# Attention plus gated MLP on one core: transposes of the next batch moved beside the output product, the MLP's first half left alone, all masks on VectorE, and a reordered start

## The chip, the cores and the metric

The kernel runs on one core of one Trainium2 chip. The metric is the device time of one execution in microseconds (us). The profile's span is 1.7 to 1.9 us shorter than the device time, because it leaves out launch and end; times inside an execution are counted from the start of that span.

A core has five engines with separate instruction queues. PE (TensorE) multiplies matrices and, against an identity matrix, transposes. DVE (VectorE) and ACT (ScalarE) do elementwise work. POOL (GpSimd) can do elementwise work too, and here it also issues nearly all loads. SP (SyncE) issues the stores. PE writes to PSUM, everything else lies in SBUF.

## The reference

Eight batches, each with eight heads of attention (576 positions, 64 numbers per head) and then one gated MLP block. Heads 0 to 3 look back over 32 positions; heads 4 to 7 over 128 positions, every fourth one.

```python
scores = q @ k.T / sqrt(64)          # masked: band of 32, or 32 steps of 4
attn   = softmax(scores) @ v         # [8, 8, 576, 64]
x      = heads side by side          # [8, 576, 512]
h      = gelu(x @ w_in)              # [8, 576, 1024]
u, v   = h[..., :512], h[..., 512:]
v_n    = layernorm(v) * g_ln
v_s    = w_sg @ v_n + b_sg           # mixes the 576 positions
out    = x + (u * v_s) @ w_out
```

## The kernel before

One batch is worked on per pass `p`, and the gate and the output product of batch `p-1` are woven in. The stages are written as strings that set the program order of every engine. `S:h` is scores, exp and mask of a head. `sgu` is the gate product, its scaled result `vs` and the product `gat`. `AV` is the weighted sum with its normalised result `onorm`. `X` transposes `onorm` into `xT`. `out` is the output product. `T:g` transposes q and k of two heads of the next batch into `qT` and `kT` (`kI` for the dilated heads). `zv` and `zu` are the two halves of `x @ w_in`. `vn` normalises. `W` transposes w_sg, in pass 0 only.

```python
        # a_S, the end of a head's scores
        nc.scalar.activation(PT[:, 0:S]..., pss[:, :, 0:HS], AF.Exp, scale=0.125)
        eng = nc.gpsimd if b and h % 4 == 3 else nc.vector      # masks of heads 3, 7 on POOL
        eng.tensor_tensor(PT[:, 0:S], PT[:, 0:S], masks[:, h // 4], AO.mult)
        ...
        # m_sgu, the end of a gate product
        nc.vector.scalar_tensor_tensor(vs..., pv[:, :, 0:HS], g_col[:, ph:ph + 1], b_bc..., AO.mult, AO.add)
        nc.vector.tensor_tensor(gat[:, ph, :], u[:, ph, :], vs, AO.mult)
        ...
        # m_zv, after gelu: statistics on DVE, then 1/sqrt(var) as rs on POOL
        nc.gpsimd.tensor_scalar_add(rs[:, 0:n], mv[:, 0:n, 1:2], 1e-6)
        nc.gpsimd.tensor_tensor(rs[:, 0:n], rs[:, 0:n], mhalf[:, 0:n], AO.pow)
        ...
    for p in range(B + 1):
        ...
        # io: loads, spread evenly between the steps of a string
        run("S:0 sgu:0 S:1 S:2 sgu:1 S:3 S:4 sgu:2 S:5 sgu:3 S:6 S:7 gelu", env, io)
        ...
        run("AV:0 vd AV:1 out:0 X:0 AV:2 X:1 out:1 AV:3 X:2 T:0 X:3 out:2", env, io)
        ...
        run("zv:0 T:1 zv:1 vn:0 W:0 T:2 zv:2 vn:1 W:1 zu:0 vn:2 T:3 zu:1 W:2 zu:2 W:3 zu:3 W:4", env, io)
```

All PSUM results share one pool of four slots, so a result that is copied out late also holds up a later product. The weight transposes, the first q and k, and all loads of pass 0 are written before or inside the same strings.

The softmax here doesn't subtract the row's maximum and nothing guards it: scores larger than these inputs give would overflow.

Of the kernel before, what the change touches and what calls it, by code (L numbers as in the profile page):

```python
# [11 lines left out]
FP16 = mybir.dt.float16  # L12
AF = mybir.ActivationFunctionType
AO = mybir.AluOpType

B, H, S, D = 8, 8, 576, 64
DM, DFF, DH = 512, 1024, 512
# [8 lines left out]
NB, QB, KB, HALO = 6, 96, 128, 32  # L26
# [27 lines left out]
def kernel(  # L54
# [12 lines left out]
    nc = tc.nc  # L67
# [6 lines left out]
    sb = ctx.enter_context(tc.tile_pool(name="sb", bufs=2))  # L74
# [7 lines left out]
    masks = const.tile([KB, 2, S], FP16)  # L82
# [7 lines left out]
    warm = const.tile([128, 1], FP32)  # L90


    NKT = 3
    kTs = [[const.tile([128, HALO + S], FP16, name=f"kT{i}_{hd}") for hd in range(2)]
           for i in range(NKT)]

# [3 lines left out]
    NV = 2  # L100
    vps = [const.tile([KB, 4, NB, 66], FP16, name=f"vp{i}") for i in range(NV)]
    vds = [const.tile([KB, 4, NB, 66], FP16, name=f"vd{i}") for i in range(NV)]
    NPT = 10
    PTb = [const.tile([KB, PTW], FP16, name=f"PT{i}") for i in range(NPT)]

    def setup_consts():
        nc.sync.dma_start(ident16, IDT.ap())
        nc.sync.dma_start(masks, MSK.ap())
        nc.vector.memset(mhalf, -0.5)
        for i in range(NKT):  # L110
            for hd in range(2):
                nc.vector.memset(kTs[i][hd], 0.0)
            nc.vector.memset(kIs[i], 0.0)
        for t in vps + vds:
            nc.vector.memset(t[0:HALO], 0.0)
            nc.vector.memset(t[:, :, :, 64:65], 1.0)
        for t in PTb:
            nc.vector.memset(t[:, S:PTW], 1.0)
        nc.vector.memset(wsgT16[0:64, 4, :], 0.0)


    def dma(dst, src):
        nc.gpsimd.dma_start(dst, src)  # L123

    loaded = {}

    def open_batch(b):
        qp = ld.tile([QB, NB, 4, D], FP16, tag="qp", name="qp")
        kp = ld.tile([QB, NB, 4, D], FP16, tag="kp", name="kp")
        qd = ld.tile([TB, 4, 2, 4, D], FP16, tag="qd", name="qd")  # L130
        kd = ld.tile([TB, 4, 2, 4, D], FP16, tag="kd", name="kd")
        loaded[b] = ((qp, kp), (qd, kd))

    def ld_plain(b, h0):
        if h0 == 0:
            open_batch(b)
        for t, src in zip(loaded[b][0], (q, k)):
            for h in range(h0, h0 + 2):
                dma(t[:, :, h, :], src[b][h].rearrange("(a p) d -> p a d", p=QB))

    def ld_dil(b):
        for t, src in zip(loaded[b][1], (q, k)):
            dma(t.rearrange("p h f r d -> p (h f) (r d)"),
                src[b][4:8].rearrange("h (f p r) d -> p (h f) (r d)", p=TB, r=4))
# [24 lines left out]
        nc.vector.tensor_copy(vd[:, :, 4:6, 0:D], vt[:, :, 0:3:2, :])  # L169

    def ld_win():
        dma(w_in16, moe_w_in.rearrange("(g p) f -> p g f", p=128))

    def ld_wsg():
        dma(wsg16, moe_w_sg.rearrange("(a p) s -> p a s", p=QB))
# [51 lines left out]
    def a_S(b, h):  # L227
        qT, kT = qkT[b, h // 2]
        pss = psum("pss")
        if h < 4:  # L230
            kx, qx = kT[h % 2], qT.rearrange("p j w -> p (j w)")
            for a in range(NB):
                nc.tensor.matmul(pss[:, a // 3, QB * (a % 3):QB * (a % 3) + QB],
                                 kx[:, QB * a:QB * a + KB], qx[:, QB * a:QB * a + QB],
                                 start=True, stop=True)
        else:
            for j in range(2):
                kx = kT[:, h % 2, NM * j:NM * j + NM, :]
                qx = qT[:, h % 2, NM * j:NM * j + NM]
                for r in range(2):  # L240
                    nc.tensor.matmul(pss[:, j, 128 * r:128 * r + 128],
                                     kx[:, 0:KB, r], qx[:, 0:128], start=True, stop=True)
                nc.tensor.matmul(pss[:, j, 256:HS], kx[:, NM - 64:NM, :],  # L243
                                 qx[:, 128:NM].unsqueeze(1).broadcast_to([128, 2, 16]),
                                 start=True, stop=True)
        PT = PTb[(8 * b + h) % NPT]
        nc.scalar.activation(PT[:, 0:S].rearrange("p (j w) -> p j w", j=2),  # L247
                             pss[:, :, 0:HS], AF.Exp, scale=0.125)
        eng = nc.gpsimd if b and h % 4 == 3 else nc.vector
        eng.tensor_tensor(PT[:, 0:S], PT[:, 0:S], masks[:, h // 4], AO.mult)  # L250
        PTs[b, h] = PT

    def a_AV(b, g):
# [23 lines left out]

    def a_X(b, g):
        onorm = onorms.pop((b, g))
        if g == 0:  # L280
            xTs[b] = sb.tile([128, 4, S], FP16, tag="xT", name="xT", bufs=4)
        xT = xTs[b]
        pxt = psum("pxt")
        if g < 2:
# [21 lines left out]
    def m_zv(b, i):  # L306
# [10 lines left out]
                                 start=(g4 == 0), stop=(g4 == 3))  # L317
        vv = sb.tile([128, 2, DH], FP32, tag="vv", name="vv", bufs=3)
        nc.scalar.activation(vv[:, 0:n], pz[:, 0:n], AF.Gelu_apprx_tanh)  # L319
        st = sb.tile([128, 2, 6], FP32, tag="st", name="st", bufs=3)  # L320
        mv = sb.tile([128, 2, 2], FP32, tag="mv", name="mv", bufs=3)
        rs = sb.tile([128, 2, 1], FP32, tag="rs", name="rs", bufs=3)
# [63 lines left out]
    def gelu_table():  # L386
        nc.scalar.activation(warm, mhalf[:, 0, :], AF.Gelu_apprx_tanh)

    LOADS = {"qk": lambda b: [(ld_plain, b, 0), (ld_plain, b, 2), (ld_dil, b)],
             "v": lambda b: [(ld_vp, b, 0, 4), (ld_vd, b)]}  # L390

    def run(text, env, io):

        steps = text.split()
        done = 0
        for i, step in enumerate(steps):
            while done < len(io) and done * len(steps) <= i * len(io):
                f, *a = io[done]
                f(*a)
                done += 1  # L400
            name, _, n = step.partition(":")
            if name in env:
                f, *a = env[name]
                f(*a, *([int(n)] if n else []))
        for f, *a in io[done:]:
            f(*a)

    setup_consts()
    for f, *a in LOADS["qk"](0) + LOADS["v"](0):
        f(*a)  # L410
    ld_win()
    for g in range(4):
        a_T(0, g)
    for p in range(B + 1):
        env = {"gelu": (gelu_table,)}
        if p < B:
            env |= {"S": (a_S, p), "AV": (a_AV, p), "X": (a_X, p), "vd": (cp_vd, p),
                    "zv": (m_zv, p), "vn": (m_vn, p), "zu": (m_zu, p)}
        if p + 1 < B:
            env["T"] = (a_T, p + 1)  # L420
        if p == 0:
            env["W"] = (prep_wsg,)
        if p >= 1:
            env |= {"sgu": (m_sgu, p - 1), "out": (m_out, p - 1)}
        if p == 0:
            io = LOADS["qk"](1) + [(ld_wsg,)]
        else:
            io = LOADS["v"](p + 1) if p + 1 < B else []
        run("S:0 sgu:0 S:1 S:2 sgu:1 S:3 S:4 sgu:2 S:5 sgu:3 S:6 S:7 gelu", env, io)
        io = LOADS["v"](1) + [(ld_wout,)] if p == 0 else []  # L430
        run("AV:0 vd AV:1 out:0 X:0 AV:2 X:1 out:1 AV:3 X:2 T:0 X:3 out:2", env, io)
        io = LOADS["qk"](p + 2) if p + 2 < B else []
        run("zv:0 T:1 zv:1 vn:0 W:0 T:2 zv:2 vn:1 W:1 zu:0 vn:2 T:3 zu:1 W:2 zu:2 W:3 zu:3 W:4",
            env, io)


# [28 lines left out]
```

## Time and profile before

| | before |
|---|---|
| device time, median (range) | 289.38 us (289.23 to 290.4) |
| span of the profile | 287.8 us |
| pass 0: start to the first scores of pass 1 | 52.89 us |
| a steady pass (first scores to next first scores) | 31.70 us |
| from the first scores of the last attention pass to the end | 45.64 us |

Two sections of the profile page of the kernel before follow: the span with each engine's busy time (its share, and after x its instructions), and the span cut into 40 slices of 7.2 us, in which a digit is the busy share in tenths and PEclk the granted TensorE clock in tenths.

```profile
span 287.8 us, 6135 instructions
PE 234.7 (82%) x2494; PEld 167.4 (58%) x2494; DVE 198.7 (69%) x380; ACT 179.2 (62%) x265; POOL 138.9 (48%) x189
...
PE   0467957898889798888889898879889889888883
...
PEclk9998777999999999999999999999999999999998
```

PE is busy most of the time from the eighth slice on, but never wholly. The first seven slices look different: PE is at 0 to 9 tenths and its clock at 7 to 9. So there are two things to read, the start and a steady pass.

What PE waits for in one steady pass of the kernel before (from 115.56 to 147.26 us) is shown by the view of waits. Its columns are the waiting engine and result, what released it, the total, the count and the longest, in us.

```profile
PE pv L357 <- DVE vn L334: 1.1, 1, 1.1
PE pz L315 <- DVE kT L224: 0.9, 1, 0.9
PE pxt L286 <- ACT xT L289: 0.7, 1, 0.7
PE po L374 <- DVE vs L361: 0.4, 1, 0.4
PE po L374 <- DVE gat L364: 0.3, 1, 0.3
...
```

With two of 0.2 us that are left out, the waits sum to 3.8 us of 31.70. The largest is for `vn` before the first gate product. The second is the copy of a transposed `kT` that holds up `zv`. The third to fifth stand around the output product.

The view of instruction groups, kept apart by shape, has the products that matter on DVE and POOL. Its columns are line, engine, operation, out<-in, count, busy us and mean ns, then idle time before and what ended it.

```profile
L364 DVE TENSOR_TENSOR gat<-u,vs 128x576 f16<-128x576 f16 x32 | 23.2, 724 | 1.4
L250 DVE TENSOR_TENSOR PT<-PT,masks 128x576 f16<-128x576 f16 x50 | 21.9, 452 | 4.1 <-ACT PT L247 3.3
L250 POOL TENSOR_TENSOR PT<-PT,masks 128x576 f16<-128x576 f16 x14 | 17.8, 1273 | 18.2 <-ACT PT L247 18.2
```

A `gat` is the same size as a mask product on DVE, yet takes 724 ns on the mean against 452. The mean hides two kinds. This is the DVE timeline of one steady pass before, with start and duration in us:

```profile
119.75 0.46 DVE L364 TENSOR_TENSOR gat<-u,vs 128x576 f16<-128x576 f16 x1
...
121.71 1.20 DVE L364 TENSOR_TENSOR gat<-u,vs 128x576 f16<-128x576 f16 x1
...
125.63 1.08 DVE L364 TENSOR_TENSOR gat<-u,vs 128x576 f16<-128x576 f16 x1
```

And this is POOL's timeline of the same stretch, where a bracket gives the idle time before:

```profile
121.32 1.28 POOL L250 TENSOR_TENSOR PT<-PT,masks 128x576 f16<-128x576 f16 x1 [0.67 <-ACT PT L247]
...
125.12 1.27 POOL L250 TENSOR_TENSOR PT<-PT,masks 128x576 f16<-128x576 f16 x1 [0.52 <-ACT PT L247]
```

Two `gat` of four take 0.46 us. The two that take 1.20 and 1.08 us run while POOL multiplies a mask. A mask on POOL thus costs DVE more (0.74 and 0.62 us) than the 0.44 to 0.46 us that DVE would need for that mask itself.

### The profile page before, as it was taken

To read this page: it belongs to the slowest core of one execution; us is meant where nothing else is said; L and a number is where in the kernel's file an instruction comes from. 1 tells how busy PE (TensorE), PEld (TensorE's weight loads), DVE (VectorE), ACT (ScalarE), POOL (GpSimd) and SP (SyncE) were. 2 spreads that over 40 slices of the span, in tenths; PEclk is the share of its full clock that TensorE was granted. 3 is DMA by queue.
4 is the path that set the end of the run, shared out by engine and by line. 5 is a ranking of instruction groups with operands and counts; after the bars stand their busy time and mean duration, and the time that the engine had idled before them with its cause. 6 is when DMAs were issued, how large, how long until landed. Compare 5 with 4: busy or idle time off the path is not lost.

```text
span 287.8 us, 6135 instructions
## 1 busy us (share of the span) xinstructions
PE 234.7 (82%) x2494; PEld 167.4 (58%) x2494; DVE 198.7 (69%) x380; ACT 179.2 (62%) x265; POOL 138.9 (48%) x189
## 2 busy tenths in 40 slices
PE   0467957898889798888889898879889889888883
PEld 0366634766468466666567656756566647754652
DVE  7548347795579839794679748993879557973760
ACT  1366643656786478756787478665876678745502
POOL 8953828481188606890198407970396013200400
PEclk9998777999999999999999999999999999999998
DMA  9999999998169921997079923995099310012004
GB/s 129 133 190 150 155 183 108 103 107 151 53 43 126 184 99 8 95 159 171 18 48 156 156 93 25 108 147 155 16 69 164 122 57 2 2 73 93 0 0 164
DMA packets 91467, 28.92 MB, mean 100 GB/s; under 512 B 71664, under 2 KB 86064, under 8 KB 91440
## 3 DMA queue, kind: packets, MB, share of 16 engines
q0 software_dynamic: 85232, 18.48, 72.3%
q1 hardware_dynamic: 6208, 10.06, 10.3%
q8 instruction: 19, 0.31, 0.4%
q14 instruction: 8, 0.07, 0.1%
HBM read 37.54 MB, written 9.44 MB: 163 GB/s over the span
## 4 chain that ended last, share of the span: by engine, by line
DVE 31%; PE 30%; ACT 13%; DMA 10%; POOL 8%; issue 6%; POOLq 0%; ACTq 0%; DVEq 0%
PE po L374 8%; PE pu L344 8%; DVE vs L361 7%; PE pz L315 7%; DVE gat L364 5%; DVE st L324 5%; DMA w_in<-in_moe_w_in_dram 4%; DVE PT L250 4%; DMA wsg<-in_moe_w_sg_dram 4%; DVE onorm L273 3%; ACT vv L319 3%; POOL kp L123 2%; ACT u L347 2%; PE po L377 2%; ACT osb L380 2%
## 5 line engine op out<-in xcount | busy, mean ns | idle before, releaser
L326 POOL TENSOR_SCALAR rs<-mv 128x2 f32<-128x2 f32 (+1 forms) x24 | 7.2, 300 | 96.8 <-DVE mv L325 96.1
L357 PE MATMUL pv<-wsgT,vn 128*128 128x288 f16 x320 | 45.4, 286 | 7.3 <-DVE vn L334 6.3
L247 ACT ACTIVATE PT<-pss 128x576 f16<-128x576 f32 x64 | 38.5, 650 | 16.5 <-PE pss L243 9.9
L374 PE MATMUL po<-w_out,gat 128*128 128x512 f16 x160 | 42.6, 379 | 5.6 <-DVE gat L364 3.0
L324 DVE BATCH_NORM_STATS2 st<-vv 128x6 f32<-128x512 f32 x40 | 27.2, 681 | 25.2 <-ACT vv L319 24.8
L315 PE MATMUL pz<-w_in,xT 128*128 128x512 f16 x160 | 39.9, 392 | 5.6 <-DVE kT L224 5.6
L380 ACT COPY osb<-po 128x1024 f32<-128x1024 f32 (+1 forms) x24 | 20.9, 870 | 37.4 <-issue 20.9
L357 PEld LDWEIGHTS <-vn 128*128 128x128 f16 x320 | 29.0, 97 | 16.2 <-DVE vn L334 8.6
L344 PE MATMUL pu<-xT,w_in 128*128 128x288 f16 x256 | 35.7, 294 | 2.6 <-ACT u L347 1.6
L344 PEld LDWEIGHTS <-w_in 128*128 128x128 f16 x256 | 25.7, 100 | 11.6 <-issue 3.7
L334 DVE TENSOR_SCALAR vn<-vv,mv,rs 128x512 f16<-128x512 f32 x40 | 22.1, 584 | 13.8 <-POOL rs L327 13.8
L273 DVE TENSOR_TENSOR onorm<-poa,rc 96x768 f16<-96x768 f32 (+1 forms) x32 | 30.6, 956 | 1.1
L319 ACT ACTIVATE vv<-pz 128x1024 f32<-128x1024 f32 (+1 forms) x24 | 21.1, 882 | 14.0 <-PE pz L315 11.6
L347 ACT ACTIVATE u<-pu 128x576 f16<-128x576 f32 x32 | 20.8, 651 | 13.2 <-PE pu L344 13.1
L123 POOL DMA_DIRECT2D qp<-in_q_dram x32 | 25.1, 786 | 6.8 <-DMA wsg<-in_moe_w_sg_dram 3.7
L215 ACT CAST qT<-pq 128x576 f16<-128x576 f32 x32 | 20.4, 638 | 12.3 <-PE pq L204 6.4
L123 POOL DMA_DIRECT2D kp<-in_k_dram x32 | 23.9, 752 | 7.8 <-DMA w_in<-in_moe_w_in_dram 4.1
L315 PEld LDWEIGHTS <-xT 128*128 128x128 f16 x160 | 15.3, 101 | 20.9 <-issue 7.5
L361 DVE SCALAR_TENSOR_TENSOR vs<-pv,g_col,b_bc 128x576 f16<-128x576 f32 x32 | 25.9, 811 | 1.2 <-PE pv L357 1.0
L250 POOL TENSOR_TENSOR PT<-PT,masks 128x576 f16<-128x576 f16 x14 | 17.8, 1273 | 18.2 <-ACT PT L247 18.2
L374 PEld LDWEIGHTS <-gat 128*128 128x128 f16 x160 | 14.4, 100 | 18.9 <-DVE gat L364 7.2
L250 DVE TENSOR_TENSOR PT<-PT,masks 128x576 f16<-128x576 f16 x50 | 21.9, 452 | 4.1 <-ACT PT L247 3.3
(65 smaller groups left out, 442.1 us busy)
## 6 DMA issues: line engine op xcount, KB each, us to landing
out_dram<-osb SPq DMA_DIRECT2D x32, 256.0 KB, 2.3
qp<-in_q_dram POOLq DMA_DIRECT2D x32, 72.0 KB, 3.9
kp<-in_k_dram POOLq DMA_DIRECT2D x32, 72.0 KB, 3.4
qd<-in_q_dram POOLq DMA_DIRECT2D x8, 288.0 KB, 5.5
kd<-in_k_dram POOLq DMA_DIRECT2D x8, 288.0 KB, 6.5
vp<-in_v_dram POOLq DMA_DIRECT2D x8, 288.0 KB, 8.4
vm<-in_v_dram POOLq DMA_DIRECT2D x8, 256.0 KB, 6.5
vt<-in_v_dram POOLq DMA_DIRECT2D x16, 96.0 KB, 6.1
```

The costliest lines, as they stand in the source:

```text
L123: nc.gpsimd.dma_start(dst, src)
L247: nc.scalar.activation(PT[:, 0:S].rearrange("p (j w) -> p j w", j=2), pss[:, :, 0:HS], AF.Exp, scale=0.125)
L250: eng.tensor_tensor(PT[:, 0:S], PT[:, 0:S], masks[:, h // 4], AO.mult)
L273: nc.vector.tensor_tensor(onorm.rearrange("p a h d -> p h a d"), pv[:, :, :, 0:64], rc.unsqueeze(3).broadcast_to([rows, 2, NB, 64]), AO.mult)
L315: nc.tensor.matmul(pz[:, c, :], xT[:, g4, MT[ti]:MT[ti] + 128], w_in16[:, g4, DH:DFF], start=(g4 == 0), stop=(g4 == 3))
L319: nc.scalar.activation(vv[:, 0:n], pz[:, 0:n], AF.Gelu_apprx_tanh)
L324: nc.vector.bn_stats(st[:, c, :], vv[:, c, :])
L344: nc.tensor.matmul(pu[:, j, 0:HS], w_in16[:, g4, 128 * ph:128 * ph + 128], xT[:, g4, HS * j:HS * j + HS], start=(g4 == 0), stop=(g4 == 3))
L357: nc.tensor.matmul(pv[:, j, 0:HS], vn[:, kp, 128 * ph:128 * ph + 128], wsgT16[:, kp, HS * j:HS * j + HS], start=(kp == 0), stop=(kp == 4))
L361: nc.vector.scalar_tensor_tensor(vs.rearrange("p (j w) -> p j w", j=2), pv[:, :, 0:HS], g_col[:, ph:ph + 1], b_bc.rearrange("p (j w) -> p ...
L374: nc.tensor.matmul(po[:, c, :], gat[:, ph, ts], w_out16[:, ph, :], start=(ph == 0), stop=False)
L380: nc.scalar.copy(osb[:, 0:n], po[:, 0:n])
```

## The change

Its intent: put every transpose of the next batch into the stage of the output product, so that the MLP's first half runs without them; take all masks from POOL; split the statistics from `zv`, so that they stand two tiles ahead of the normalisation; place each load by hand; and start faster, with the loads of large packets (the dilated heads) first, w_in in two halves, and w_sg's transposes last in pass 0.

```diff
-    NKT = 3
+    NKT = 2
-    NPT = 10
+    NPT = 8
 ... (fewer and smaller memsets; xT bufs 4 -> 2)
     def ld_win():
-        dma(w_in16, moe_w_in.rearrange("(g p) f -> p g f", p=128))
+        for half in (slice(DH, DFF), slice(0, DH)):
+            dma(w_in16[:, :, half], moe_w_in[:, half].rearrange("(g p) f -> p g f", p=128))
 ...
-        eng = nc.gpsimd if b and h % 4 == 3 else nc.vector
-        eng.tensor_tensor(PT[:, 0:S], PT[:, 0:S], masks[:, h // 4], AO.mult)
+        nc.vector.tensor_tensor(PT[:, 0:S], PT[:, 0:S], masks[:, h // 4], AO.mult)
 ...
+        norm[b, i] = (vv, tis)
+
+    def m_st(b, i):
+        vv, tis = norm.pop((b, i))
 ... (statistics as before, now a step of their own)
-    for f, *a in LOADS["qk"](0) + LOADS["v"](0):
+    for f, *a in [(ld_dil, 0), (ld_vd, 0), (ld_plain, 0, 0), (ld_plain, 0, 2),
+                  (ld_vp, 0, 0, 4), (ld_win,), (ld_plain, 1, 0), (ld_plain, 1, 2), (ld_dil, 1), (ld_wsg,)]:
         f(*a)
-    ld_win()
-    for g in range(4):
-        a_T(0, g)
 ... (LV, LVd, LP, LD: loads of v, of dilated v, of plain and of dilated q and k)
+            run("""T0:2 T0:3 S:4 S:5 S:6 S:7 vd T0:0 AV:2 T0:1 AV:3 S:0 X:2 S:1 X:3 S:2 S:3
+                   AV:0 AV:1 gelu X:0 X:1
+                   zv:0 st:0 zv:1 st:1 vn:0 zv:2 st:2 vn:1 LV LVd wout zu:0 vn:2 zu:1 T:0 zu:2
+                   T:1 zu:3 T:2 T:3 W:0 W:1 W:2 W:3 W:4 LP:0 LP:2 LD""", env)
+            continue
-        run("S:0 sgu:0 S:1 S:2 sgu:1 S:3 S:4 sgu:2 S:5 sgu:3 S:6 S:7 gelu", env, io)
-        run("AV:0 vd AV:1 out:0 X:0 AV:2 X:1 out:1 AV:3 X:2 T:0 X:3 out:2", env, io)
-        run("zv:0 T:1 zv:1 vn:0 W:0 T:2 zv:2 vn:1 W:1 zu:0 vn:2 T:3 zu:1 W:2 zu:2 W:3 zu:3 W:4",
-            env, io)
+        run("S:0 S:1 sgu:0 S:2 S:3 sgu:1 S:4 S:5 sgu:2 S:6 sgu:3 S:7 gelu", env)
+        run("""vd AV:0 LV AV:1 LVd T:0 out:0 LD X:0 AV:2 X:1 T:1 LP:0 out:1 AV:3 X:2 T:2 LP:2 X:3 T:3
+               out:2""", env)
+        run("zv:0 st:0 zv:1 st:1 vn:0 zv:2 st:2 vn:1 zu:0 vn:2 zu:1 zu:2 zu:3", env)
```

More of the change, by code (lines that the diff above doesn't have):

```diff
@@ L108, in setup_consts @@
         nc.sync.dma_start(masks, MSK.ap())
-        nc.vector.memset(mhalf, -0.5)
         for i in range(NKT):
@@ L112, in setup_consts @@
                 nc.vector.memset(kTs[i][hd], 0.0)
-            nc.vector.memset(kIs[i], 0.0)
-        for t in vps + vds:
-            nc.vector.memset(t[0:HALO], 0.0)
-            nc.vector.memset(t[:, :, :, 64:65], 1.0)
+        for t in kIs:
+            nc.vector.memset(t, 0.0)
+        for i in range(NV):
+            nc.vector.memset(vps[i][0:HALO, 0, 0, 0:D], 0.0)
+            nc.vector.memset(vps[i][:, :, :, D:D + 1], 1.0)
+            nc.vector.memset(vds[i][:, :, :, D:D + 1], 1.0)
         for t in PTb:
             nc.vector.memset(t[:, S:PTW], 1.0)
+        nc.vector.memset(mhalf, -0.5)
         nc.vector.memset(wsgT16[0:64, 4, :], 0.0)
@@ L127, in open_batch @@
     def open_batch(b):
+        if b in loaded:
+            return
         qp = ld.tile([QB, NB, 4, D], FP16, tag="qp", name="qp")
@@ L134, in ld_plain @@
     def ld_plain(b, h0):
-        if h0 == 0:
-            open_batch(b)
+        open_batch(b)
         for t, src in zip(loaded[b][0], (q, k)):
@@ L141, in ld_dil @@
     def ld_dil(b):
+        open_batch(b)
         for t, src in zip(loaded[b][1], (q, k)):
@@ L279, in a_X @@
         onorm = onorms.pop((b, g))
-        if g == 0:
-            xTs[b] = sb.tile([128, 4, S], FP16, tag="xT", name="xT", bufs=4)
+        if b not in xTs:
+            xTs[b] = sb.tile([128, 4, S], FP16, tag="xT", name="xT", bufs=2)
         xT = xTs[b]
@@ L319, in m_zv @@
         nc.scalar.activation(vv[:, 0:n], pz[:, 0:n], AF.Gelu_apprx_tanh)
+        norm[b, i] = (vv, tis)
+    def m_st(b, i):
+        vv, tis = norm.pop((b, i))
+        n = len(tis)
         st = sb.tile([128, 2, 6], FP32, tag="st", name="st", bufs=3)
@@ L387, in gelu_table, with run @@
         nc.scalar.activation(warm, mhalf[:, 0, :], AF.Gelu_apprx_tanh)
-    LOADS = {"qk": lambda b: [(ld_plain, b, 0), (ld_plain, b, 2), (ld_dil, b)],
-             "v": lambda b: [(ld_vp, b, 0, 4), (ld_vd, b)]}
-    def run(text, env, io):
-        steps = text.split()
-        done = 0
-        for i, step in enumerate(steps):
-            while done < len(io) and done * len(steps) <= i * len(io):
-                f, *a = io[done]
-                f(*a)
-                done += 1
+    def run(text, env):
+        for step in text.split():
             name, _, n = step.partition(":")
@@ L404, in run @@
                 f(*a, *([int(n)] if n else []))
-        for f, *a in io[done:]:
-            f(*a)
     setup_consts()
-    for f, *a in LOADS["qk"](0) + LOADS["v"](0):
+    for f, *a in [(ld_dil, 0), (ld_vd, 0), (ld_plain, 0, 0), (ld_plain, 0, 2),
+                  (ld_vp, 0, 0, 4), (ld_win,), (ld_plain, 1, 0), (ld_plain, 1, 2), (ld_dil, 1), (ld_wsg,)]:
         f(*a)
-    ld_win()
-    for g in range(4):
-        a_T(0, g)
     for p in range(B + 1):
@@ L417 @@
             env |= {"S": (a_S, p), "AV": (a_AV, p), "X": (a_X, p), "vd": (cp_vd, p),
-                    "zv": (m_zv, p), "vn": (m_vn, p), "zu": (m_zu, p)}
+                    "zv": (m_zv, p), "st": (m_st, p), "vn": (m_vn, p), "zu": (m_zu, p)}
         if p + 1 < B:
-            env["T"] = (a_T, p + 1)
-        if p == 0:
-            env["W"] = (prep_wsg,)
+            env |= {"T": (a_T, p + 1), "LV": (ld_vp, p + 1, 0, 4), "LVd": (ld_vd, p + 1)}
+        if p + 2 < B:
+            env |= {"LP": (ld_plain, p + 2), "LD": (ld_dil, p + 2)}
         if p >= 1:
@@ L425 @@
         if p == 0:
-            io = LOADS["qk"](1) + [(ld_wsg,)]
-        else:
-            io = LOADS["v"](p + 1) if p + 1 < B else []
-        run("S:0 sgu:0 S:1 S:2 sgu:1 S:3 S:4 sgu:2 S:5 sgu:3 S:6 S:7 gelu", env, io)
-        io = LOADS["v"](1) + [(ld_wout,)] if p == 0 else []
-        run("AV:0 vd AV:1 out:0 X:0 AV:2 X:1 out:1 AV:3 X:2 T:0 X:3 out:2", env, io)
-        io = LOADS["qk"](p + 2) if p + 2 < B else []
-        run("zv:0 T:1 zv:1 vn:0 W:0 T:2 zv:2 vn:1 W:1 zu:0 vn:2 T:3 zu:1 W:2 zu:2 W:3 zu:3 W:4",
-            env, io)
+            env |= {"T0": (a_T, 0), "W": (prep_wsg,), "wout": (ld_wout,)}
+            run("""T0:2 T0:3 S:4 S:5 S:6 S:7 vd T0:0 AV:2 T0:1 AV:3 S:0 X:2 S:1 X:3 S:2 S:3
[7 more added lines that the diff above has]
+        run("zv:0 st:0 zv:1 st:1 vn:0 zv:2 st:2 vn:1 zu:0 vn:2 zu:1 zu:2 zu:3", env)
 _INS = ['q', 'k', 'v', 'moe_w_in', 'moe_g_ln', 'moe_w_sg', 'moe_b_sg', 'moe_w_out']
```

## The prediction

> **What bounds it now.** The timeline shows a batch every 31.70 us, from `zv` to the next `zv` (72.76, 104.46, 136.16 us). In such a period the windows view has PE busy 27.8, DVE 23.7, ACT 22.3 us, clock 1.00, DMA share 0.87. Matmul issue intervals read from the PE timeline sum to about 26.1 us, so some 5.5 us are stalls. The largest: 1.09 for `vn`, 0.93 before `zv:2` for the DVE half of `kT`, 0.66 before the second `X`, 0.36+0.31 for `gat`. From the first exp to the first output product DVE is the limit: 8.52 busy of 8.70 us. The start is separate: pass 0 reaches `zv` at 31.1 us (pass 1: 72.8, so 10 us more than a period between), under DMA waits (w_in lands 25.9, wsg 39.1) and a granted clock of 0.67 to 0.84 between 20 and 50 us.
>
> **What changes, costed.**
> 1. Masks on DVE: POOL loses 14 x 1.27 us; DVE gains 0.88 us per batch (2 x 0.44), but the two `gat` that meet POOL's mask take 1.20 and 1.08 us, the others 0.46: net about -0.5 us DVE per batch. "Advanced Engine Details and Errata", VectorE Performance Modes (Trainium skill), says GpSimd and two-port Vector instructions block each other; the trace agrees.
> 2. MLP's first half alone: the `kT` wait (0.93) and three transposes of 0.5 us leave it. POOL's rs no longer waits behind DMA issues. The before kernel's last batch already runs in this order: there `vn` ends 10.1 us after `zv` began, so a wait of about 0.9 us before `sgu:0` stays.
> 3. Transposes beside the output product: they fill the time in which PE waits for `gat`, but add PSUM users and ACT/DVE copies there. I walked one period by hand with the trace's durations and the built program's PSUM slots: the first mask starts 11 us after `zv` (now 14), the output product waits about 0.8 us for the gelu table load and the first `qT` copy, smaller waits remain. Estimate: 31.0 to 31.4 us per period, a small gain. The last batch but for the tail has no transposes left: about 28 us instead of 31.0. The tail (25.7) stays.
> 4. Start: dilated loads (large packets) first, w_in's v half first, wsg's transposes last. PE starts near 6.5 us, `zv` near 23; then wsg (still about 38 us, same bytes ahead of it) gates pass 1, with five wsgT copies of 0.76 us after it: `sgu:0` near 43 to 44 us (now 53.9), pass-1 `zv` near 64.5 instead of 72.8.
>
> **Sum (estimates).** 64.5 + 5 x 31.2 + 28 + 25.7 + 1.5 launch = 275.7. I predict 276 us, -4.6%; range 269 to 283.5. Faster by over 2%: 0.88; within: 0.11; slower: 0.01. Most of it comes at the start (8 us) and in the last pass (3 us).
>
> **What would show it.** Pass-1 `zv` at 62 to 68 us; steady period 30.6 to 31.8; no `kT` wait at `zv`, no POOL entry for PT, `gat` mean near 0.46 us; a wait of 0.7 to 1.0 us for `vn` before `sgu:0`; DVE gapless from first mask to fourth transposed `kT`; PE waits before `out` for ACT's `qT` or `xT`; last batch's period near 28.
>
> **What would make it wrong.** Wsg landing late or DMA of batch 2 (queued at pass 0's end) missing pass 1's transposes; the dense second stage serialising on the four PSUM slots (period up by 1 us: 281); or a period of 30 (270).

## The result, and the profile after

The kernel after takes 280.56 us (280.08 to 281.08), against 289.38 us before. The ratio is 0.9688, with a 95% interval of 0.9659 to 0.9717, so 3.1% faster. A ratio here and below is the mean time of one kernel's fast runs over that of the other's in the same rounds, so it is not quite the ratio of the medians quoted. The result is correct.

The same sections of the page, for the kernel after (a slice is now 7.0 us):

```profile
span 278.6 us, 6139 instructions
PE 233.1 (84%) x2494; PEld 167.0 (60%) x2494; DVE 188.8 (68%) x387; ACT 177.6 (64%) x265; POOL 122.7 (44%) x176
...
PE   0386988978988898979988898989988998989883
...
PEclk9999795999999999999999999999999999999999
```

DVE took on 14 masks and is nevertheless busy for 9.9 us less. The groups by shape show a part of the reason; the two lines answer to the three of before:

```profile
L254 DVE TENSOR_TENSOR PT<-PT,masks 128x576 f16<-128x576 f16 x64 | 27.7, 453 | 8.4 <-ACT PT L252 7.5
L373 DVE TENSOR_TENSOR gat<-u,vs 128x576 f16<-128x576 f16 x32 | 14.7, 458 | 1.4
```

The masks cost 5.8 us more on DVE, and `gat` costs 8.5 us less, which is 2.7 of the 9.9 us. By the same view the memsets, fewer and smaller now, take about 4 us less, and `vn` about 2 us less. What PE waits for in one steady pass after (108.74 to 139.90 us):

```profile
PE pv L366 <- DVE vn L343: 0.7, 1, 0.7
PE pk L209 <- DVE vs L370: 0.6, 1, 0.6
PE po L383 <- ACT xT L305: 0.5, 1, 0.5
PE poa L270 <- DVE onorm L277: 0.5, 1, 0.5
PE po L383 <- ACT qT L220: 0.4, 1, 0.4
...
```

The wait for `kT` at `zv` is gone, the one for `vn` is shorter, and the sum (with two of 0.3 and 0.2 us that are left out) is 3.2 us instead of 3.8. But the four lines below the first are new, and they all stand in the stage that took the transposes. `pk <- vs` is a transpose that waits for a PSUM slot until DVE, as it computes `vs`, has read it. `po <- qT` and `po <- xT` are the output product waiting for ACT's copies.

Where the 9.2 us of span went, counted from the first scores of a pass to the next:

| | before | after | gain |
|---|---|---|---|
| pass 0, to the first scores of pass 1 | 52.89 | 46.75 | 6.14 |
| passes 1 to 6 | 189.27 | 186.17 | 3.10 (0.52 each) |
| the rest | 45.64 | 45.68 | 0.0 |

Two thirds of the gain is the start, one third is spread over six passes, and the end gains nothing.

### The profile page after: what moved, and what is told of

Its sections match the earlier page's. It is cut to its first block, busy times and chain, and to the rows that moved or that the text cites. A ratio compares the mean times of both kernels' runs of the same rounds, so it can differ in the third digit from the quotient of the medians.

```text
span 278.6 us, 6139 instructions
## 1 busy us (share of the span) xinstructions
PE 233.1 (84%) x2494; PEld 167.0 (60%) x2494; DVE 188.8 (68%) x387; ACT 177.6 (64%) x265; POOL 122.7 (44%) x176
## 4 chain that ended last, share of the span: by engine, by line
DVE 39%; PE 26%; ACT 20%; issue 7%; DMA 4%; POOL 1%; POOLq 0%; ACTq 0%; DVEq 0%
PE pz L319 9%; PE po L383 8%; DVE vs L370 8%; DVE PT L254 6%; DVE st L333 6%; DVE onorm L277 5%; DVE gat L373 4%; DMA vm<-in_v_dram 3%; ACT PT L252 3%; DVE vn L343 3%; ACT L252 3%; ACT osb L389 3%; PE pu L353 3%; ACT xT L305 2%; PE pv L366 2%
## 5 line engine op out<-in xcount | busy, mean ns | idle before, releaser
L335 POOL TENSOR_SCALAR rs<-mv 128x2 f32<-128x2 f32 (+1 forms) x24 | 8.6, 357 | 101.8 <-DVE mv L334 101.8
L366 PE MATMUL pv<-wsgT,vn 128*128 128x288 f16 x320 | 46.3, 289 | 5.8 <-DVE vn L343 5.2
L383 PE MATMUL po<-w_out,gat 128*128 128x512 f16 x160 | 41.5, 379 | 9.3 <-ACT qT L220 3.4
L319 PE MATMUL pz<-w_in,xT 128*128 128x512 f16 x160 | 37.7, 392 | 0.5 <-ACT xT L293 0.5
L125 POOL DMA_DIRECT2D kp<-in_k_dram x32 | 23.6, 740 | 27.9 <-DMA qd<-in_q_dram 11.3
L254 DVE TENSOR_TENSOR PT<-PT,masks 128x576 f16<-128x576 f16 x64 | 27.7, 453 | 8.4 <-ACT PT L252 7.5
L353 PE MATMUL pu<-xT,w_in 128*128 128x288 f16 x256 | 33.0, 286 | 0.3 <-ACT u L356 0.3
L277 DVE TENSOR_TENSOR onorm<-poa,rc 128x768 f16<-128x768 f32 (+1 forms) x32 | 30.6, 955 | 1.1
L229 DVE CAST kI<-pk 64x576 f16<-64x576 f32 x16 | 12.9, 805 | 23.1 <-ACT kI L228 23.1
L125 POOL DMA_DIRECT2D qp<-in_q_dram x32 | 23.9, 763 | 4.8 <-DMA vp<-in_v_dram 2.0
L343 DVE TENSOR_SCALAR vn<-vv,mv,rs 128x512 f16<-128x512 f32 x40 | 19.9, 531 | 3.8 <-POOL rs L336 3.8
```

Of the source, the lines that this page charges most:

```text
L125: nc.gpsimd.dma_start(dst, src)
L254: nc.vector.tensor_tensor(PT[:, 0:S], PT[:, 0:S], masks[:, h // 4], AO.mult)
L277: nc.vector.tensor_tensor(onorm.rearrange("p a h d -> p h a d"), pv[:, :, :, 0:64], rc.unsqueeze(3).broadcast_to([rows, 2, NB, 64]), AO.mult)
L319: nc.tensor.matmul(pz[:, c, :], xT[:, g4, MT[ti]:MT[ti] + 128], w_in16[:, g4, DH:DFF], start=(g4 == 0), stop=(g4 == 3))
L343: nc.vector.tensor_scalar(vn[:, ti, :], vv[:, c, :], mv[:, c, 0:1], rs[:, c, :], AO.subtract, AO.mult)
L353: nc.tensor.matmul(pu[:, j, 0:HS], w_in16[:, g4, 128 * ph:128 * ph + 128], xT[:, g4, HS * j:HS * j + HS], start=(g4 == 0), stop=(g4 == 3))
```

## The experiments

The theories before the first runs were these. Mine: moving the transposes brings most of the steady gain, and the masks a little (0.1 to 0.3 us per pass). Rival 1: the masks bring it, because they no longer slow `gat`. The first runs spoke for the rival, and from run 8 on contention of POOL with DVE is called my theory. The rival there: the kernel before lost its time by waiting for masks that POOL made late. Each run below gave a correct result. The medians are of four to six fast runs; "pass" is a steady pass as counted above.

### 1. Only the masks, in the kernel before

```diff
-        eng = nc.gpsimd if b and h % 4 == 3 else nc.vector
-        eng.tensor_tensor(PT[:, 0:S], ...
+        nc.vector.tensor_tensor(PT[:, 0:S], ...
```

> The kernel before with only the masks moved to VectorE. Before and after differ by 9.24 us of span: 6.14 us until pass 1 begins, 0.52 us in each of six following passes, nothing in the tail. Rival 1 (masks): the 0.52 us per pass is the end of the slow gat (1.20 and 1.08 instead of 0.46 us) less two more masks on VectorE (0.88 us), so this kernel runs a pass in 31.2 us, total about 286 (1.1 to 1.3% faster). My theory (order): moving the transposes takes most of it; here a pass drops by 0.1 to 0.3 us, total 287.5 to 289. Under both gat falls to about 0.46 us and no mask stands on POOL.

It measured 285.59 us, ratio 0.9862 (0.9831 to 0.9892). Pass 0 stays (52.71 us), and a steady pass takes 30.89 us instead of 31.70, which is 0.81 less. That is more than the 0.52 that the whole change gained per pass. Both forecasts for the pass missed, mine (0.1 to 0.3 us less) by more than the rival's (31.2 us); the total lies near the rival's 286. The mean of `gat` is 458 ns, as in the kernel after. PE's waits in one steady pass of this kernel (114.23 to 145.12 us) are:

```profile
PE pv L356 <- DVE vn L333: 1.1, 1, 1.1
PE pz L314 <- DVE kT L224: 0.9, 1, 0.9
PE pxt L285 <- DVE onorm L272: 0.8, 2, 0.7
PE pu L343 <- ACT u L346: 0.2, 1, 0.2
```

They sum to 3.0 us. The waits around the output product (`gat`, `vs`) have gone, and those for `vn` and `kT`, which the rest of the change was to remove, are all still there. The pass length less these waits is 27.9 us in this kernel and in the one before, and 28.0 in the kernel after. So the other parts of the change exchanged waits of the same size.

### 2. The masks of heads 3 and 7 back on POOL, in the kernel after

```diff
-        nc.vector.tensor_tensor(PT[:, 0:S], ...
+        eng = nc.gpsimd if b and h % 4 == 3 else nc.vector
+        eng.tensor_tensor(PT[:, 0:S], ...
```

> The changed kernel with the masks of heads 3 and 7 back on POOL, as before. Rival 1 (masks): passes go back to 31.5 to 31.7 us and the total to 283.5 to 285. My theory (order): the masks are worth up to 0.3 us per pass, total 281 to 282.7. In both, two gat per pass take over 1 us again where they meet a mask on POOL.

It measured 291.32 us, ratio 1.0077 (1.0035 to 1.0119): not only the whole gain is lost, the kernel is slower than before. Both theories missed. My forecast was 281 to 282.7 us, the rival's 283.5 to 285. A steady pass takes 32.0 to 32.2 us, about 1.0 more than after, and pass 1 alone takes 36.93 us instead of 31.08. The mean of `gat` is 696 ns. What both theories left out is that POOL is also the queue that issues loads. This is POOL's timeline in pass 1 of this kernel, which begins at 47.35 us:

```profile
52.93 0.73 POOL L125 DMA_DIRECT2D kp<-in_k_dram  x1 [1.53 <-DMA w_out<-in_moe_w_out_dram]
...
54.76 0.83 POOL L125 DMA_DIRECT2D kd<-in_k_dram  x1
55.61 1.29 POOL L255 TENSOR_TENSOR PT<-PT,masks 128x576 f16<-128x576 f16 x1
```

The first mask stands at once behind the last load issue, and one of those issues had itself waited 1.53 us for an earlier load (w_out) to land. The start of the kernel after leaves more load issues for pass 1, and everything else on POOL waits in line. How the 5.9 us of pass 1 split between this, a granted clock of 0.50 there (47.35 to 52 us; 0.72 in the kernel after from 46.75 to 52) and the waits of PE that follow (1.36 and 0.91 us for `vs`, 1.49 for `onorm`) stays open.

### 3 and 4. The start alone, and the steady part alone

The third run takes the kernel after's start and pass 0, and from pass 1 on the kernel before's strings and masks. The fourth does the reverse: the old start, and from pass 1 on the new strings and masks.

```diff
 # 3: from pass 1 on
+        run("S:0 sgu:0 S:1 S:2 sgu:1 S:3 S:4 sgu:2 S:5 sgu:3 S:6 S:7 gelu", env, io)
+        run("AV:0 vd AV:1 out:0 X:0 AV:2 X:1 out:1 AV:3 X:2 T:0 X:3 out:2", env)
+        run("zv:0 st:0 T:1 zv:1 st:1 vn:0 T:2 zv:2 st:2 vn:1 zu:0 vn:2 T:3 zu:1 zu:2 zu:3", env, io)
 # 4: pass 0 as before, then the three strings of the kernel after, masks on nc.vector
```

> The changed kernel's start (loads, memsets, order of pass 0) with the old order and the old masks from pass 1 on. If start and steady state add up: pass 1 begins near 46.8 us as in the changed kernel, then passes of 31.7 us; total 289.4 - 6.1 = 283.3 (2.1% faster). If instead the start's gain is given back because loads of batch 2 arrive late, pass 1 is longer than 31.7 and the total is above 285.

> The old start (loads, memsets, order of pass 0) with the changed order and masks from pass 1 on. If the parts add up: pass 1 begins near 52.9 us as before, then passes of about 31.0 us; total 289.4 - 3.1 = 286.3 (1.1% faster). If the steady gain needs the early start (loads further ahead), the total is above 288.

The start alone measured 286.77 us (ratio 0.9904, 0.9866 to 0.9943), the steady part alone 286.22 us (0.9891, 0.9859 to 0.9923). The start alone reaches pass 1 at 46.36 us, 6.5 us earlier than before, but its pass 1 takes 33.48 us where the kernel before takes 30.97, so 2.5 us are given back at once. Its POOL masks of pass 1 run at 56.40 and 59.68 us, behind load issues that follow one another from 48.17 us on, one of them after a wait of 1.44 us for w_out. Then it runs in 31.66 us per pass, as before. No wait of PE in pass 1 is for a load, so late loads of batch 2, the reason given in the forecast, are not what lengthened it. The steady part alone has passes of 30.8 to 31.2 us and reaches pass 1 at 52.16 us.

The two parts do not just add. By medians in the same rounds (289.62 us for the kernel before), the start alone gives 2.9 us and the steady part alone 3.4, together 6.3; the whole change gave 8.8 in its own rounds. The masks alone (run 1, same rounds) gave 4.0, so the new order added nothing to them. The missing 2.5 us are as much as the start gives back in pass 1. Whether POOL's masks cause that is not shown, because a rival stands beside them: the clock. The view by windows gives, for a stretch, the busy time and count of each engine, then the granted clock, the DMA share and the GB/s. Here is the beginning of pass 1 in the kernel before, and then in run 3:

```profile
52.89:58.00 5.11, 4.82 (x61) 3.90 (x59) 3.38 (x8) 4.44 (x7) 1.15 (x3) 1.00 1.47 148
```

```profile
46.36:52.00 5.64, 5.28 (x33) 3.62 (x33) 4.32 (x8) 1.84 (x3) 3.60 (x6) 0.50 1.58 173
```

In run 3 PE does 33 products in 5.64 us at a clock of 0.50, where it did 61 in 5.11 us at 1.00. Runs 10 and 11 below, which have all masks on DVE, show what such a difference can be worth.

### 5. The transposes back in their old places

```diff
-        run("""vd AV:0 LV AV:1 LVd T:0 out:0 LD X:0 AV:2 X:1 T:1 LP:0 out:1 AV:3 X:2 T:2 LP:2 X:3 T:3
+        run("""vd AV:0 LV AV:1 LVd out:0 LD X:0 AV:2 X:1 LP:0 out:1 AV:3 X:2 T:0 LP:2 X:3
                out:2""", env)
-        run("zv:0 st:0 zv:1 st:1 vn:0 zv:2 st:2 vn:1 zu:0 vn:2 zu:1 zu:2 zu:3", env)
+        run("zv:0 st:0 T:1 zv:1 st:1 vn:0 T:2 zv:2 st:2 vn:1 zu:0 vn:2 T:3 zu:1 zu:2 zu:3", env)
```

(NKT goes back to 3 and xT to 4 buffers.)

> The changed kernel (start, loads, masks on VectorE) with the transposes of the next batch back where the old kernel has them, three of four inside the MLP half. The run with only the masks moved made a pass 30.89 us, the changed kernel makes 31.03: so the move of the transposes is worth nothing or costs a little. If so: pass 1 begins near 46.8 us, passes of 30.0 to 30.9 us (below 30.9 because no DMA issue on POOL delays the rs of tile 2 any more, which cost PE 1.1 us per pass), total 275 to 280. If the move was a gain that the masks hid: passes of 31.2 us or more, total above 281.5.

It measured 282.53 us, ratio 0.9751 (0.9717 to 0.9785). What it takes longer than the kernel after arises in the first passes (pass 1 begins 0.7 us later, and pass 2 takes 32.92 us). The steady pass takes 31.06 us, and that of the kernel after averages 31.03. I had hoped for less than 30.9, and that failed; the total even lies in the rival's range (above 281.5), though the steady pass is below its 31.2. So moving the transposes is worth nothing in a steady pass: the wait for `kT` at `zv` (0.93 us) comes back, and of the waits before `out` those for `qT` and `xT` go, but one of 0.7 us for `gat` comes.

### 6. A faster first load

```diff
-        nc.sync.dma_start(b_bc, moe_b_sg.unsqueeze(0).to_broadcast([128, S]))
+        dma(b_bc, moe_b_sg.unsqueeze(0).to_broadcast([128, S]))    # behind w_sg, on POOL's queue
```

> The changed kernel with the 288 KB bias broadcast issued on POOL behind wsg instead of on SP at once. The prediction had PE begin at 6.5 us; it began at 9.2, when qd landed. If the constants' loads take the bandwidth from qd (theory): qd lands 1.5 to 2 us sooner and the whole kernel is 1 to 2 us faster (279 to 279.5). If qd's landing is set by its own packets (rival): it lands at 9.0 to 9.3 and the time stays.

It measured 280.06 us, ratio 0.9681 (0.9655 to 0.9707), which is that of the kernel after. PE's first matmul begins at 7.83 us instead of 9.22, but pass 1 begins at 46.77 us instead of 46.75. The lead of 1.4 us had shrunk to 0.3 when `zv` began, and the rest went in the first `zv`: its last 19 matmuls take 6.50 us here and 5.96 us in the kernel after, with a granted clock of 0.50 against 0.66 between 28 and 33 us. Each forecast was right in one half: the load did land sooner, and the time did stay. The first load does not set the length of pass 0.

### 7. Two of the four transposes inside the second MLP half

```diff
-               ... AV:3 X:2 T:2 LP:2 X:3 T:3 out:2
+               ... AV:3 X:2 LP:2 X:3 out:2
-        run("zv:0 ... zu:0 vn:2 zu:1 zu:2 zu:3", env)
+        run("zv:0 ... zu:0 vn:2 zu:1 T:2 zu:2 T:3 zu:3", env)
```

> The changed kernel with two of the four transposes put between the u products. They should fill PE's 0.7 us wait for vn before the first gate product, at the price of a later exp (ACT copies before u 3). If the wait is worth filling: passes of 30.3 to 30.7 us, total 276.5 to 279. If the later exp eats it up (VectorE's chain from mask 0 on starts later): 31.0 us and no change.

It measured 283.09 us, ratio 0.9786 (0.9757 to 0.9815), and a pass of 31.34 us, worse than either place and than both forecasts. The scores of the next pass then wait 0.7 us for DVE's copy of `kI`, and the first exp begins about 12 us after `zv` instead of 10.4.

### 8. The suspected cost by itself: a POOL product that nobody reads

This is kernel 1 (all masks on DVE) with a product of a mask's size on POOL added for heads 3 and 7.

```diff
         nc.vector.tensor_tensor(PT[:, 0:S], PT[:, 0:S], masks[:, h // 4], AO.mult)
+        if b and h % 4 == 3:
+            nc.gpsimd.tensor_tensor(scr, PT[:, 0:S], masks[:, h // 4], AO.mult)
```

> The old kernel with all masks on VectorE, plus a POOL product of the same size as a mask for heads 3 and 7, whose result nobody reads. If VectorE is slowed by POOL's work at the same time (contention, my theory for the 0.81 us per pass): some gat or mask is again above 0.8 us and a pass takes 31.3 to 31.7 us. If the old kernel lost by waiting for masks that POOL made late (rival): passes stay at 30.9 us.

It measured 288.21 us, ratio 0.9967 (0.9941 to 0.9994). The pass grows from 30.89 to 31.36 us, by 0.47. Nothing waits for the added product. It could still delay `rs`, which POOL computes too, but `vn` waits for `rs` as long as without it (1.46 us, and 1.47 in kernel 1). That leaves contention. Two lines of POOL's timeline of this kernel:

```profile
121.94 1.42 POOL L252 TENSOR_TENSOR scr<-PT,masks 128x576 f16<-128x576 f16 x1 [1.98 <-DVE PT L250]
...
126.16 1.27 POOL L252 TENSOR_TENSOR scr<-PT,masks 128x576 f16<-128x576 f16 x1 [0.78 <-DVE rc L273]
```

And two of DVE's timeline in the same stretch:

```profile
122.99 0.69 DVE L366 TENSOR_TENSOR gat<-u,vs 128x576 f16<-128x576 f16 x1
...
127.06 0.66 DVE L169 COPY vd<-vm 128x1024 f16<-128x1024 f16 x1
```

The `gat` and the copy that meet the POOL product take 0.69 us and 0.66 us; the same two without it take 0.46 and 0.42. The sum, 0.23 + 0.24, is the 0.47 us by which the pass grew. The forecast for the pass held; the one for the single instruction (above 0.8 us) did not.

The end times say more than the durations. In the kernel before, all 14 `gat` that met a mask on POOL ended 0.30 to 0.33 us after that mask, wherever they had begun; here the `gat` end 0.31 to 0.32 us and the copies 0.27 to 0.29 us after the POOL product. So DVE's instruction looks held until POOL is nearly done, and not slowed by a factor: its cost depends on how much of POOL's product is still to come. `vs` and `onorm`, which read PSUM, kept their 0.81 and 0.95 us beside POOL.

### 9. A warm clock in pass 0

The granted clock fell below full in the start of every kernel. This run fills PE's idle time in pass 0 of the kernel after with throwaway products that are overwritten.

```diff
+    def heat(pt, n):
+        for _ in range(n):
+            nc.tensor.matmul(pt[:, 0, :], ident16, masks[:, 0, 0:512], start=True, stop=True)
 ... # ahead of the real products in pass 0: 14 before the first pq, 2 each before pq 2 and 3
 ... # of batch 1, 3 each before two poa, 4 and 3 before two pxt, 3 before pz, 2 each before two pw
```

> The changed kernel with throwaway matmuls (128x512, results overwritten) where PE idles in pass 0: 14 before the first transposes, 2 to 4 each before the waits for VectorE up to the first zv, and in front of the last transposes and wsg's. The bias run began 1.4 us sooner and lost the lead in the first zv, whose 20 matmuls ran at a granted clock of 0.50 to 0.66. If the cold clock is what the start lost (theory): granted clock near 1.00 from 9 us on, zv's 20 matmuls in 4.3 to 4.5 instead of 6.9 us, pass 1 begins 2 to 4 us sooner (43 to 45 us), total 276.5 to 279. If the start is bound by the copies on ACT and VectorE (rival): the clock rises, pass 1 still begins at 46 us or later, total 280 or more.

It measured 279.45 us, ratio 0.9637 (0.961 to 0.9664), between the two forecasts; the interval just touches that of the kernel after (0.9659 to 0.9717). This is the view by windows for 28 to 33 us, first of the kernel after:

```profile
28.00:33.00 5.00, 4.49 (x18) 1.64 (x16) 0.00 (x0) 1.61 (x2) 3.13 (x4) 0.66 1.27 85
```

Then the warmed kernel:

```profile
28.00:33.00 5.00, 4.97 (x29) 2.23 (x28) 0.97 (x3) 2.05 (x4) 3.12 (x4) 1.00 1.23 85
```

The clock did not stay full from 9 us on, as intended. An earlier window of the warmed kernel:

```profile
13.00:19.00 6.00, 5.09 (x51) 3.90 (x51) 4.80 (x9) 4.87 (x9) 5.85 (x8) 0.50 1.69 108
```

So the run tells what a warm clock is worth from the first `zv` on, and not before it. From 28 to 33 us PE does 29 products instead of 18 in the same 5 us. The 20 products of the first `zv` take 4.52 us; in the kernel after 19 of them took 5.96. Yet pass 1 begins only 1.0 us earlier (45.76 us). The first load landed 0.8 us later here (10.02 us) and `zv` began 1.1 us later (29.19); the products after `zv` began 1.3 us earlier than in the kernel after, and 0.3 of that was lost until pass 1. Pass 1 is 0.5 us shorter (30.58), and pass 2 gives 0.65 us back (31.56 us against 30.91).

### 10. Another order around the new waits

The waits of the kernel after suggested three moves: one more head of scores in front of the first gate product, to cover `vn`; the first output product ahead of the first transpose; and the last one ahead of the last.

```diff
-        run("S:0 S:1 sgu:0 S:2 S:3 sgu:1 S:4 S:5 sgu:2 S:6 sgu:3 S:7 gelu", env)
-        run("""vd AV:0 LV AV:1 LVd T:0 out:0 LD X:0 AV:2 X:1 T:1 LP:0 out:1 AV:3 X:2 T:2 LP:2 X:3 T:3
-               out:2""", env)
+        run("S:0 S:1 S:2 sgu:0 S:3 sgu:1 S:4 S:5 sgu:2 S:6 sgu:3 S:7 gelu", env)
+        run("""vd AV:0 LV AV:1 LVd out:0 T:0 LD X:0 AV:2 X:1 T:1 LP:0 out:1 AV:3 X:2 T:2 LP:2 X:3
+               out:2 T:3""", env)
```

> The changed kernel with three steps moved from pass 1 on: the third score product before the first gate product (to fill 0.25 of the 0.7 us wait for vn), the output product's first pair before the first transposes (these waited 0.6 us for vs and the product 0.4 us for their copy; now one wait of 0.7 us for gat is left), the last output tile before the last transposes (it waited 0.5 us for xT). If the waits are independent: 0.8 to 1.2 us off each pass, passes of 29.9 to 30.3 us, total 275 to 277. If VectorE's chain sets the pass and PE's waits only move: passes of 30.8 to 31.1, total 280 to 281.

It measured 276.82 us, ratio 0.9552 (0.9521 to 0.9584). A steady pass takes 30.29 us, 0.74 less than after. PE's waits in one such pass (107.83 to 138.12 us) are:

```profile
PE po L383 <- DVE gat L373: 0.7, 1, 0.7
PE pk L209 <- DVE rc L275: 0.4, 1, 0.4
PE pv L366 <- DVE vn L343: 0.3, 1, 0.3
PE pq L209 <- ACT xT L293: 0.3, 1, 0.3
```

They sum to 1.7 us instead of 3.2. Pass and total lie in the range of the first forecast. As first written, the new place of the transposes put about as many waits beside `out` as it took from `zv`, and three moves in the strings remove half of all waits. What each move brings was not run alone, nor the moved score with the transposes in their old places, so this doesn't show that the new place is the better one. (The length less the listed waits is 28.6 us here, so 0.6 us of the 1.5 went into something that the view of waits does not list.)

### 11 and 12. Both, and one load step moved

The eleventh run has the order of 10 and the throwaway products of 9. The twelfth also moves one load step.

```diff
-               ... out:1 AV:3 X:2 T:2 LP:2 X:3 out:2 T:3
+               ... out:1 AV:3 X:2 T:2 X:3 out:2 T:3
-        run("zv:0 st:0 zv:1 st:1 vn:0 zv:2 st:2 vn:1 zu:0 vn:2 zu:1 zu:2 zu:3", env)
+        run("zv:0 st:0 zv:1 st:1 vn:0 zv:2 st:2 vn:1 LP:2 zu:0 vn:2 zu:1 zu:2 zu:3", env)
```

> Both of the former two in one kernel. If start and steady state add up, its gain over the changed kernel is the sum of the two: at best 272 to 275, and equal to the better of them if one gives nothing.

> The kernel with both changes, with the last plain loads of the batch after next issued behind the rs of the MLP half instead of before it. In that kernel pass 1 began its S stage near 46.2 us and pass 2 at 74.9, but pass 2 then took 32.93 instead of 30.29 us: POOL issued its last kp load at 73.7 us after a wait for kd, with rs ready to be computed about 2 us before. If POOL's order is the cause: pass 2 near 30.3 to 30.8 us, steady passes unchanged at 30.3, total 272.5 to 274. If the loads of batch 3 are simply late for want of bandwidth: pass 2 stays above 32 us, total 275 to 276.

The eleventh measured 275.66 us, ratio 0.95 (0.9463 to 0.9536), just outside its forecast. Its pass 1 is short: 28.63 us, where the tenth, with the same order, takes 31.45. The beginning of pass 1, first in the tenth, then in the eleventh:

```profile
46.09:52.00 5.91, 5.71 (x38) 4.00 (x38) 4.39 (x8) 2.60 (x4) 3.77 (x6) 0.50 1.58 171
```

```profile
46.24:52.00 5.76, 5.61 (x75) 4.75 (x73) 5.35 (x11) 3.58 (x6) 2.88 (x4) 1.00 1.84 173
```

The two kernels differ by the throwaway products alone, and pass 1 differs by 2.8 us with the clock at 0.50 and at 1.00. So a cold clock can cost in pass 1 as much as the start alone gave back in run 3 (2.5 us), with no mask on POOL at all. These are readings of one profiled execution each, and the clock there is not fixed by the program: the kernel after has the same pass 0 as the tenth, and read 0.72. Pass 2 of the eleventh takes 32.93. POOL's timeline of this kernel shows what happened at the turn from pass 1 to pass 2:

```profile
71.27 0.73 POOL L125 DMA_DIRECT2D kp<-in_k_dram  x1 [2.57 <-DMA qd<-in_q_dram]
73.68 0.72 POOL L125 DMA_DIRECT2D kp<-in_k_dram  x1 [1.69 <-DMA kd<-in_k_dram]
74.48 0.23 POOL L345 TENSOR_SCALAR rs<-mv 128x2 f32<-128x2 f32 x1
```

Two load issues wait 2.57 and 1.69 us for earlier loads to land, and `rs`, a product of 256 numbers without which DVE can't normalise, stands behind them; its input had been ready since about 71.3 us. With the loads moved behind it, in the twelfth kernel, `rs` waits only for its input:

```profile
71.19 0.23 POOL L345 TENSOR_SCALAR rs<-mv 128x2 f32<-128x2 f32 x1 [4.26 <-DVE mv L344]
```

That kernel measured 273.66 us (272.51 to 274.23), ratio 0.9425 (0.939 to 0.9459). Its pass 1 takes 29.38 us and all steady ones 30.29. It is the fastest kernel: 5.75% faster than before, and by its median, taken in other rounds, about 2.5% below the kernel after.

## Why the prediction was right or wrong

The total fell inside the range (276 predicted, 269 to 283.5; measured 280.56), and the direction was right, but one step of the start failed, and another came out by luck. The gain was put at 4.6% and was 3.1%. The prediction was a sum of five terms, so it can be checked term by term (in the profiled run of 280.37 us):

| term | predicted | measured | difference |
|---|---|---|---|
| `zv` of pass 1 begins | 64.5 | 69.59 | +5.1 |
| five passes, `zv` to `zv` | 5 x 31.2 = 156.0 | 155.09 | -0.9 |
| last batch | 28 | 28.03 | 0.0 |
| tail | 25.7 | 25.89 | +0.2 |
| launch | 1.5 | 1.77 | +0.3 |
| sum | 275.7 | 280.4 | +4.7 |

**The start (item 4) was mis-sized, and it is the whole miss.** The prediction had PE start near 6.5 us, `zv` near 23, `sgu:0` near 43 to 44 and `zv` of pass 1 near 64.5. They came at 9.22, 28.10, 48.08 and 69.59 us. The last is outside the 62 to 68 us that the prediction itself named as its sign; `zv` of pass 1 began at 72.60 in the kernel before, so 3.0 us were gained at this mark and not 8. This is PE's timeline of the kernel after at those points:

```profile
9.22 0.66 PE L216 MATMUL pq<-ident,qd 72*128 72x72 f16 x8 [9.22 <-DMA qd<-in_q_dram]
...
28.10 0.38 PE L319 MATMUL pz<-w_in,xT 128*128 128x512 f16 x1
29.00 5.96 PE L319 MATMUL pz<-w_in,xT 128*128 128x512 f16 x19 [0.51 <-ACT xT L293]
...
48.08 2.16 PE L366 MATMUL pv<-wsgT,vn 128*128 128x288 f16 x10
```

All 5 us were lost before the first `zv`: PE began 2.7 us late, and from there to `zv` it took 18.9 us, where the prediction's own marks leave 16.5. This stretch is the step that failed. Starting PE sooner does not repair it, for run 6 removed 1.4 us of the delay and only 0.3 us was left at `zv`. What the trace shows in the stretch are waits of PE for 5.1 us in all: 1.55 us until `kd` has landed, and 0.25 to 0.75 us each for DVE's `kI`, `vd`, `PT` and (three times) `onorm`. How the 2.4 us beyond the prediction divide among them stays open: no run removes one alone. The clock may have a part too, for the transposes of six products took 0.64 to 0.68 us up to 19.1 us and 0.42 later, but run 9 does not test it, because its clock was 0.50 there as well (13 to 19 us).

From `zv` to `sgu:0` the prediction's marks leave 20 to 21 us, and it took 19.98. That was luck, for the reason given was wrong. The landing of w_sg was to gate pass 1, but no product waits for it in the kernel after (in the kernel before PE waited 2.90 us). What filled the stretch instead was the first `zv` at a clock of 0.66 and the copies after it; the first gate product took 2.16 us too, and 1.39 in later passes. Run 9, with the clock at 1.00, takes 16.6 us from `zv` to the scores of pass 1, where the kernel after takes 18.7. The prediction names a clock of 0.67 to 0.84 in the kernel before, but has no term for it in the new start.

**The steady pass (31.0 to 31.4) was right in size and wrong in its reason.** It measured 31.0. The prediction gave the masks about 0.5 us of DVE time per batch and counted on a small gain from the transposes. Run 1 shows that the masks alone are worth 0.81 us per pass, and run 5 that the move of the transposes is worth nothing (31.03 with it, 31.06 without). The statement about contention itself held. The prediction cites "Advanced Engine Details and Errata", VectorE Performance Modes (Trainium skill), where GpSimd and two-port Vector instructions are said to block each other. The table there lists no two-port mode for tensor_tensor, which `gat` is, so that rule does not cover it. The better reference is "GPSIMD Engine Reference", 1. Specifications (Trainium skill), whose row on SBUF interfaces adds DVE instructions with two SBUF inputs, as `gat` is. This agrees: `gat` took 0.46 us alone and, in steady passes, 0.68 to 1.38 us beside a POOL product, and run 8 shows the cost with nothing depending on that product.

**The MLP's first half alone (item 2) did what was said.** The `kT` wait left `zv`, and a `vn` wait of 0.7 us stayed, as predicted (0.7 to 1.0). But the split of the statistics from `zv` changed no order at all on DVE. In the last batch, where both kernels have no transposes, the sequence of statistics and normalisations is the same, and takes 7.05 us in both (264.96 to 272.01 us before, 255.74 to 262.79 after).

**The transposes beside the output product (item 3)** brought the predicted waits for `qT` (0.43 us) and `xT` (0.53). DVE was not gapless up to the fourth `kT`, though: it is so up to the first one, and then stands idle for 0.99, 0.94, 1.26 and 0.93 us. The "last pass (3 us)" was partly a matter of counting. From `zv` to `zv` the last batch did fall from 31.03 to 28.03 us, but the transposes only moved to the other side of the mark. Counted from the last batch's first scores to the first gate product of the tail, that length was 28.01 us before and is 28.03 after.

**What the prediction did not see** is that its parts depend on each other. With masks on POOL, pass 1 after the early start is 2.5 us longer (run 3, against the kernel before) and 5.9 us longer (run 2, against the kernel after). In both the masks stand behind load issues, because POOL issues the loads and does not get to a mask or to `rs` while an issue waits. But in both the clock was 0.50 as well at the beginning of pass 1; between runs 10 and 11 such a difference went with 2.8 us. Item 2 said that `rs` would no longer wait behind load issues. In the steady passes of the kernel after it doesn't; runs 11 and 12 show that once the start is fast this depends on where the loads are placed.

Four things stay open: how the excess of pass 1 in runs 2 and 3 divides between POOL's queue and the clock; which part of the new start (order of loads, smaller memsets, order of the strings) brings its 6 us, since run 3 tests it only as a whole; where the 2.4 us before the first `zv` went; and why a steady pass of run 1 (30.89 us) is 0.14 us shorter than that of the kernel after (its listed waits are 3.0 us against 3.2).

## What to carry to other kernels

Before work is handed to a second engine to relieve the first, read from the timeline how long the first one's instructions take while the helper runs: here a helper of 1.27 us per mask cost more than the mask, because two instructions per pass were held until it was nearly done. When work is moved out of one stage, list the waits of the stage that receives it; if they sum to as much as was removed, the order around the new waits is the next thing to change; here three such moves were worth 0.74 us per pass, and the first move nothing. On an engine that also issues loads, put small urgent work ahead of the issues.

## What the Trainium skill lacked or had wrong

- "Advanced Engine Details and Errata", VectorE Performance Modes, names only two-port modes as conflicting with GPSIMD, which is too narrow: `gat`, a tensor_tensor with two SBUF inputs, went from 0.46 to 0.69 us beside an unread POOL product, and to 1.08 and 1.20 us beside POOL's masks. "GPSIMD Engine Reference", 1. Specifications, has the wider rule. In steady passes the runs show 0.2 to 1.1 us added to a DVE instruction of 0.42 to 0.46 us.
- "TensorE: Matmul & The Clock Gate", Part 1, What's actually happening, says that the default is throttled and activity releases it. The warmed pass 0 agrees (clock 1.00 instead of 0.66 between 28 and 33 us). The section puts the penalty of the ramp below 1% of a typical span. Here the clock was low again later (0.66 in 28 to 33 us and 0.70 in 40 to 47 of the kernel after), and run 9 was 1.1 us of 280.56 faster, which is 0.4%: it agrees for the span, but the first `zv` alone took 5.96 us for 19 products instead of 4.52 for 20, and pass 1 took 31.45 us in run 10 and 28.63 in run 11. The section Seeing it yourself warns of the clock records, and rightly: in the kernel after the column reads 1.00 from 9 to 29 us, although transposes of six products took 0.64 to 0.68 us up to 19.1 us and 0.42 from 36 us on. In run 9 column and durations agree (0.50 from 13 to 19 us, with 0.64 to 0.68 us in that time). So durations are the better witness.
- "ScalarE: Activation LUTs", What ACT_TABLE_LOAD costs, adds a drain of about 1380 ns to a load of about 1283 ns. The load agrees (1.28 us), but no such drain shows: in the kernel after an activation ended at 78.68 us, the load began at 78.69 and the next exp at 79.99.
- No page that I read tells what load issues cost the small products behind them on POOL: `rs` began at 74.48 us in run 11, after issues that had waited 2.57 and 1.69 us, and at 71.19 us in run 12, where one load step stood behind it.
